# A long convolution inside a gated mixer: one 2048-point plan against two halves of 1024 with three spectrum products

## The chip, the cores and the metric

The kernel runs on one core of one Trainium2 chip. The core has a matrix engine (PE, whose weight loads are shown apart as PEld), a vector engine (DVE), an activation engine (ACT), a general engine (POOL) and an engine that mostly issues transfers (SP). The metric is the time of one execution in microseconds (us), the median of several runs.

## The reference, cut to what matters

A sequence of 2048 rows with 576 channels is normalised. One branch is a long convolution per channel, with a kernel of 2048 taps that is a sum of 128 decaying complex exponentials. The other branch is an MLP with 4608 hidden units. The product of the two is added to the input.

```python
xn = _layernorm(x, axis=-1)
# A: K[d, l] = 2 Re sum_n C[d, n] exp(A[d, n] dt[d] l),  l = 0..2047
Kf = jnp.fft.rfft(K, L2)                  # L2 = 2 * 2048
Uf = jnp.fft.rfft(u_t, L2)                # u_t = xn, transposed to (channel, time)
y = jnp.fft.irfft(Uf * Kf[None], L2)[:, :, :L]
s = y + xn * D_skip
# B: MLP with w1 (576 x 4608), w2 (4608 x 576)
g = _silu(gelu(_layernorm(xn) @ w1 + b1) @ w2 + b2)
return x + s * g
```

## The kernel before, in words

**The MLP** is the larger part of the matrix work. It runs in 48 slots (12 groups of 384 hidden units, two blocks of 512 rows, two halves of the sequence). Each slot has three first-layer units (`layer1`, line 547, 14 matmuls of 512 columns each) and eight second-layer units (`layer2`, line 604, matmuls of 288 columns). Operands are split in a high and a low part, so that three products give nearly full precision. The hidden units pass through ACT (lines 580 and 583) and DVE (line 586, tile `hl`) before the second layer can read them; DVE also adds the second layer's sums into `acc` (line 612) and makes the low parts of the weights (line 524). These matmuls use the PSUM tiles `mxa` and `mxb`, two banks each.

**The convolution** goes over the channels in six chunks of 96. It uses the other four banks, as two tiles named `cv`.

- The kernel's taps come from tables: for 16 channels at a time (36 times), `tables` builds the exponentials on DVE and ACT from packed parameters `par` (lines 822 to 882; the phases are 128 x 1040 elements, from 65 positions and 16 channels), and `kgen` (line 921) multiplies them on PE into `kt`.
- `k1` (line 1022) and `x1` (line 991) are the first transform stage, of the kernel's taps and of the input `xc`. Each runs twice in a chunk, for 48 channels. `k1` is eight matmuls with 32 rows and 128 columns of weights, 384 columns of data, in four row groups, two matmuls after another in each. `x1` is four matmuls of 64 rows by 128 columns, in two row groups, again two in each. Both fill four banks; DVE empties them with four 32 x 32 block transposes (lines 1027 and 1000), 12 channels at a time.
- `s2` (line 1049) is the second stage, four times a chunk, with matrices `f2t` loaded by SP from the scratch tensor `f2q`. It leaves two halves of the spectrum. ACT copies the kernel's spectrum to `kk` (line 1058); `prod` (line 1064) multiplies each half of the input's spectrum with the same half of the kernel's, in two DVE instructions of 384 columns, and `sums` (lines 1070 and 1071) makes complex products of them in two instructions of 192 columns. This happens twice for each `s2`: 48 sets in all.
- `inverse` (line 1093, twice a chunk, matrices `g2t`), `back` (line 1104) and `i1` (line 1119, matrix `g1t`) transform back; ACT copies the result and POOL stores it to `s_s` (line 1128).

An fp32 matmul shows as two instructions in the profile, each with its weight load.

**Preparation.** Before the first chunk, POOL, DVE and ACT turn the constant matrices into the wanted layout: `load_consts`, `load_turns` and `odd_rows` (first-stage matrices), `order_f2`, `load_f2` and `store_f2` (second stage: 16 ACT copies, line 331, between loads and stores through `f2p` and `f2q`; stores at line 336), and `order_mats` (32 small transfers, line 314, for the inverse). The chunk's first step waits for the mark `f2s` 7, the last of these stores, for `odd`, for the packed parameters, and for three tables.

**What sets the order.** `Order` is a planner in the program itself. It keeps a clock for each engine, with a written-down duration for each step, and puts the convolution's steps, tables and loads between those of the MLP. Each MLP step on ACT and DVE has a due time, and another step goes in only if it ends before the next due time. The order so made is then pinned: each engine executes in that order. A PE step of the convolution goes in after an MLP unit, when the planner's clock says that its inputs are there. One `kgen` may ride with another convolution stage (`ride`). Chunk steps are also spaced by `pace`, which aims at an end at 1060 of the planner's clock.

**The end.** `combine` (lines 641 to 653) works off the first half of the rows, channels 0 to 383 after chunk 3, and the rest after chunk 5; `last_x` and `last_s` (line 664) load what `finish` (lines 678 to 696) needs for the last eight row blocks.

Of the kernel before, what the change touches and what calls it, by code (L numbers as in the profile page):

```python
# [9 lines left out]
F32 = mybir.dt.float32  # L10
# [16 lines left out]
NV = 65  # L27
NM = 96
E1, E8, E64, E512 = 2, 10, 18, 26
# [178 lines left out]
def mixer_kernel(ctx, tc, u, log_a_real, a_imag, c_real, c_imag, log_dt, d_skip, w1, b1, w2, b2,  # L208
# [29 lines left out]
    f2p = dr.tile([P, 32 * P], F32, name="f2p")  # L238
    f2q = dr.tile([P, 32, 2, 32], F32, name="f2q")
    g2p = dr.tile([P, 8, 2, 2, 2, 32], F32, name="g2p")  # L240
    turns_s = dr.tile([2, 32], F32, name="turns_s")
# [8 lines left out]
    f1t = sb.tile([P, 2, 2, 64], F32, name="f1t")  # L250
    g1t = sb.tile([P, 32, 2], F32, name="g1t")
# [6 lines left out]
    TMP = {}  # L258

    def load_tv():  # L260
        nc.sync.dma_start(tv[:, :33], dram(tvals, 0, [[0, P], [1, 33]]))
        nc.sync.dma_start(tv[:, 33:], dram(tvals, 0, [[0, P], [1, 32]]))

    def load_consts(g):
        if g == 0:
            m = sb.tile([P, 2, 2, CH], F32, name="kk").rearrange("p a b c -> p (a b c)")
            for k, (n, w) in dict(e=(0, 64), t=(64, 64), s=(128, 32), c=(160, 2), o=(192, 128), m=(320, 32),
                                  g=(352, 32)).items():
                TMP[k] = m[:, n:n + w]
            nc.gpsimd.dma_start(dram(turns_s, 0, [[1, 32], [32, 2]]), dram(f2, 32 * 32 * P, [[P, 32], [64, 2]]))  # L270
        r = slice(32 * g, 32 * g + 32)
        h, ri = divmod(g, 2)
        nc.gpsimd.dma_start(TMP["e"][r].rearrange("p (k m) -> p k m", k=2),
                            f1[r].rearrange("p (k m) -> p k m", k=8)[:, g::4, :])
        for k, t in ((ri, TMP["g"]), (1 - ri, TMP["s"])):
            nc.gpsimd.dma_start(t[r], g1[64 * k + 32 * h:64 * k + 32 * h + 32, 32 * h:32 * h + 32])
        nc.gpsimd.dma_start(dsk[32 * g:32 * g + 1, :].rearrange("p (c m) -> p c m", m=12),
                            dram(d_skip, 12 * g, [[0, 1], [48, D // 48], [1, 12]]))

    def load_turns():  # L280
        nc.gpsimd.dma_start(TMP["t"], dram(turns_s, 0, [[0, P], [1, 64]]))
        for g in range(4):
            nc.gpsimd.dma_start(TMP["c"][32 * g:32 * g + 32], dram(turns_s, 0, [[1, 32], [32, 2]]))

    def odd_rows():

        e, t, sw, c, o, m, ev = (TMP[k] for k in "etscomg")
        V = nc.vector  # L290
        k = lambda x: x.rearrange("p (r k) -> p r k", r=2)
        V.tensor_mul(k(o[:, :64]), k(e), bc(t[:, :32], 1, 2))
        V.tensor_mul(m, e[:, 32:], t[:, 32:])
        V.tensor_sub(o[:, :32], o[:, :32], m)
        V.tensor_mul(m, e[:, :32], t[:, 32:])
        V.tensor_add(o[:, 32:64], o[:, 32:64], m)
        V.tensor_scalar(o[:, 64:], o[:, :64], -1.0, None, op0=OP.mult)
        for g in range(4):
            r = slice(32 * g, 32 * g + 32)
            V.tensor_copy(f1t[r, g % 2], bc(e[r], 1, 2))  # L300
            V.tensor_copy(f1t[r, 1 - g % 2].rearrange("p a b -> p (a b)"), o[r])
        V.tensor_scalar(c[64:], c[64:], -1.0, None, op0=OP.mult)
        for g in (0, 2):
            r = slice(32 * g, 32 * g + 32)
            V.tensor_scalar(c[r, 1:], c[r, 1:], -1.0, None, op0=OP.mult)
        V.tensor_scalar(sw, sw, c[:, 1:], None, op0=OP.mult)
        V.tensor_copy(g1t[:, :, 0], ev)
        V.scalar_tensor_tensor(g1t[:, :, 1], ev, c[:, :1], sw, op0=OP.mult, op1=OP.add)

    def order_mats(j):  # L310
        hi, ri, half = j // 4, j // 2 % 2, j % 2
        for q in (2 * half, 2 * half + 1):
            for part in range(2):
                nc.gpsimd.dma_start(g2p[32 * q:32 * q + 32, :, hi, ri, part], dram(
                    g2, (64 * ri + hi) * 32 * P + q * P + 64 * part, [[2 * 32 * P, 32], [4 * P, 8], [1, 32]]))

    def order_f2(f):
        for ri in range(2):
            nc.gpsimd.dma_start(f2p[64 * f + 32 * ri:64 * f + 32 * ri + 32, :], f2[64 * ri:64 * ri + 32, :])

    F2 = {}

    def load_f2(k):
        x = sb.tile([P, 2, 2, 2, 64], F32, name="g2t", bufs=2).rearrange("p a b c d -> p (a b c d)")
        nc.gpsimd.dma_start(x, f2p[:, 4 * k * P:4 * (k + 1) * P])

        def part(f):
            if f == 0 and k % 2 == 0:
                F2[0] = sb.tile([P, 8, 64], F32, name="f2t").rearrange("p k (r m) -> p k r m", r=2)
            r = slice(64 * f, 64 * f + 64)  # L330
            nc.scalar.activation(F2[0][r, k % 2 * 4:k % 2 * 4 + 4],
                                 x.rearrange("p (k r m f) -> p f k r m", k=4, r=2, f=2)[r, f], AF.Copy)
        return part

    def store_f2(k):
        nc.gpsimd.dma_start(f2q[:, 4 * k:4 * k + 8], F2[0])

# [1230 lines left out]
```

## Time and profile before

| | |
|---|---|
| median of three runs | 1129.78 us (1127.95 to 1130.93) |
| the profiled execution | span 1127.8 us from the first to the last instruction; its own time is not given apart from that |
| PE busy | 1106.5 us |
| PEld busy | 954.9 us |
| DVE busy | 879.0 us |
| ACT busy | 667.8 us |
| POOL busy | 183.7 us |

Busy times are those of the profile: one execution, taken by the hardware profiler. A matmul's duration in it contains a part in which the next one already runs, so that the sum of the durations of a group is far above its busy time where matmuls run side by side in the array.

### The profile page before, as it was taken

Reading aid. Unit: us, or ns where it says so; the run is one execution under the profiler, and the core shown is the slowest. Engines: PE = TensorE matmul, PEld = TensorE weight load, DVE = VectorE, ACT = ScalarE, POOL = GpSimd, SP = SyncE. Lnnn points to the kernel's source line nnn. Section 1 sums busy time; section 2 is a strip of 40 time slices with the busy share of each in tenths; the row PEclk is TensorE's granted clock in tenths of the full one; section 3 lists DMA queues with packets and bytes.
Section 4 is the critical chain, followed back from the end, with each engine's and each line's share of the span. In section 5 each row is a group of like instructions: output and inputs, shape, how many; then the busy total and the mean of one; then the engine's idle time right before and its main releaser. Section 6 shows DMA issues by size and latency. Waiting matters only on the chain.

```text
span 1127.8 us, 26832 instructions
## 1 busy us (share of the span) xinstructions
PE 1106.5 (98%) x11355; PEld 954.9 (85%) x11355; DVE 879.0 (78%) x1477; ACT 667.8 (59%) x1016; POOL 183.7 (16%) x256
## 2 busy tenths in 40 slices
PE   8999999999999999999999999999999999999997
PEld 7888989988888888878888788888887888889896
DVE  7687578799999889889988779998998465544456
ACT  6486589976667566656777736774657133242333
POOL 5447201134102000010110100000001001122300
PEclk9999999999999999999999999999999999999999
DMA  8535635635454233243351421522232335363413
GB/s 247 207 128 146 214 132 182 190 94 124 131 148 142 59 104 71 86 103 104 125 140 42 105 67 57 128 76 62 88 87 80 103 116 147 92 188 109 132 52 85
DMA packets 110809, 132.39 MB, mean 117 GB/s; under 512 B 59669, under 2 KB 77921, under 8 KB 110113
## 3 DMA queue, kind: packets, MB, share of 16 engines
q1 hardware_dynamic: 95728, 79.59, 25.6%
q0 software_dynamic: 14400, 50.20, 14.1%
q8 instruction: 89, 1.46, 0.5%
q10 hardware_dynamic: 560, 0.89, 0.3%
q14 instruction: 32, 0.25, 0.1%
HBM read 101.87 MB, written 36.63 MB: 123 GB/s over the span
## 4 chain that ended last, share of the span: by engine, by line
PE 80%; DVE 10%; DMA 5%; issue 2%; ACT 2%; POOL 0%; SPq 0%; DVEq 0%; ACTq 0%; POOLq 0%
PE mxb L604 18%; PE mxa L604 18%; PE mxa L547 17%; PE mxb L547 16%; PE cv L921 3%; PE cv L1049 3%; PE cv L1093 2%; DMA par<-par_s 2%; PE cv L1022 2%; PE cv L1119 2%; PE cv L991 1%; DVE acc L612 1%; DMA f2p<-in_f_dram 1%; DVE hl L586 1%; DVE w2l L524 1%
## 5 line engine op out<-in xcount | busy, mean ns | idle before, releaser
L586 DVE TENSOR_TENSOR hl<-h,hh 128x512 fp32r<-128x512 f32 x144 | 98.5, 688 | 134.6 <-ACT hh L583 134.2
L604 PE MATMUL mxa<-w2h,hh 128*128 128x288 f32 x573 | 171.4, 299 | 1.7 <-DVE acc L612 1.3
L604 PE MATMUL mxb<-w2h,hh 128*128 128x288 f32 x576 | 171.8, 298 | 0.1
L604 PE MATMUL mxa<-w2h,hl 128*128 128x288 f32 x573 | 169.7, 296 | 2.0 <-DVE hl L586 1.8
L604 PE MATMUL mxb<-w2h,hl 128*128 128x288 f32 x576 | 170.0, 295 | 0.5 <-DVE hl L586 0.4
L604 PE MATMUL mxb<-w2l,hh 128*128 128x288 f32 x576 | 169.6, 294 | 0.0
L604 PE MATMUL mxa<-w2l,hh 128*128 128x288 f32 x573 | 168.7, 294 | 0.0
L580 ACT ACTIVATE h<-mxa,b1t 128x512 f32<-128x512 f32 x73 | 50.1, 688 | 147.0 <-PE mxa L547 143.3
L604 PEld LDWEIGHTS mxa<-w2h,hh 128*128 128x128 f32 x573 | 107.6, 188 | 9.5 <-issue 3.9
L604 PEld LDWEIGHTS mxb<-w2h,hh 128*128 128x128 f32 x576 | 108.1, 188 | 7.8 <-issue 2.7
L604 PEld LDWEIGHTS mxa<-w2h,hl 128*128 128x128 f32 x573 | 107.5, 188 | 3.5 <-DVE hl L586 3.5
L604 PEld LDWEIGHTS mxb<-w2l,hh 128*128 128x128 f32 x576 | 108.2, 188 | 0.7
L604 PEld LDWEIGHTS mxb<-w2h,hl 128*128 128x128 f32 x576 | 108.1, 188 | 0.7 <-DVE hl L586 0.7
L604 PEld LDWEIGHTS mxa<-w2l,hh 128*128 128x128 f32 x573 | 107.6, 188 | 0.6
L822 POOL DMA_DIRECT2D par<-par_s x36 | 27.4, 763 | 429.2 <-DVE mg L865 428.3
L527 ACT ACTIVATE w2h<-raw 128x576 fp32r<-128x576 f32 x72 | 44.9, 676 | 85.9 <-PE mxa L604 85.2
L583 ACT ACTIVATE hh<-h 128x512 fp32r<-128x512 f32 x144 | 90.5, 630 | 3.7
L580 ACT ACTIVATE h<-mxb,b1t 128x512 f32<-128x512 f32 x71 | 48.9, 689 | 69.5 <-PE mxb L547 67.6
L612 DVE TENSOR_TENSOR acc<-mxb,acc 128x576 f32<-128x576 f32 x88 | 66.1, 751 | 24.8 <-PE mxb L604 24.3
L612 DVE TENSOR_TENSOR acc<-mxa,acc 128x576 f32<-128x576 f32 x88 | 65.8, 748 | 24.6 <-PE mxa L604 24.4
L547 PE MATMUL mxa<-XH,w1h 128*128 128x512 f32 x284 | 78.7, 399 | 1.3 <-DVE acc L612 1.3
L547 PE MATMUL mxb<-XH,w1h 128*128 128x512 f32 x280 | 78.6, 402 | 1.2 <-ACT h L580 1.1
(249 smaller groups left out, 2436.6 us busy)
## 6 DMA issues: line engine op xcount, KB each, us to landing
raw<-in_B_w_dram SPq DMA_DIRECT2D x72, 288.0 KB, 3.6
raw<-in_B_w_dram SPq DMA_DIRECT2D x96, 192.0 KB, 3.0
par_s<-A POOLq DMA_DIRECT2D x4, 2160.0 KB, 8.4
par<-par_s POOLq DMA_DIRECT2D x36, 240.0 KB, 4.3
f2t<-f2q SPq DMA_DIRECT2D x24, 256.0 KB, 3.6
g2t<-g2p SPq DMA_DIRECT2D x24, 256.0 KB, 3.8
raw<-in_B_w_dram SPq DMA_DIRECT2D x48, 96.0 KB, 4.2
xc<-xn_s SPq DMA_DIRECT2D x48, 96.0 KB, 3.9
```

The costliest lines, as they stand in the source:

```text
L527: nc.scalar.activation(h, r, AF.Copy)
L547: nc.tensor.matmul(q, a, b, start=j == 0, stop=j == len(ops) - 1)
L580: nc.scalar.activation(t, q, AF.Gelu_apprx_tanh, bias=b1t[:, g * G + i:g * G + i + 1], scale=1.0)
L583: LAST[0] = nc.scalar.activation(hh[:, i], t, AF.Copy)
L586: nc.vector.tensor_sub(hl[:, i], t, hh[:, i].bitcast(F32))
L604: nc.tensor.matmul(q[:, dh, :288], a[:, i, c], b[:, i, d], start=i == 0 and k == 0, stop=i == G - 1 and k == 2)
L612: nc.vector.tensor_add(o, q[:, dh:dh + n, :288], b if g == 0 else o)
L822: nc.gpsimd.dma_start(PAR[b].rearrange("p (g i) k -> p g (i k)", g=4), dram(par_s, (b // 3 * 48 + b % 3 * 4) * NPAR, [[D * NPAR, P], [12 * ...
L921: nc.tensor.matmul(q[32 * g:32 * g + 32, i // 2, i % 2 * 64:i % 2 * 64 + 64], U[:, ri, 4 * g + i, :], v[:, ri, 4 * g + i, :], start=ri == ...
L1022: nc.tensor.matmul(Q[g // 2 * 2][:, g % 2], f1t[r, (e + g) % 2].rearrange("p f k -> p (f k)"), KT[c, i][r, :, 32 * e:32 * e + 32], start=e ...
L1049: nc.tensor.matmul(Q[i][32 * q:32 * q + 32, f, 2 * ri:2 * ri + 2], m[r, 4 * i + q, 32 * ri:32 * ri + 32], A2[r, 4 * p + 2 * i + q // 2, :, ...
L1093: nc.tensor.matmul(QI[q // 2][64 * f:64 * f + 64, q % 2, i], MAT["g2t", p + i // 2][r, i % 2, f, ri], YS[p + i // 2][0][r, i % 2, ri, f], ...
```

## The change

The sequence is split in two halves of 1024, input and kernel alike. Each half is transformed by itself, 32 by 32 points, with all frequencies shifted by a quarter, so that the part of a product that runs over the end of the half comes out as the imaginary part. The first half of the result is the real part of (input half 0 times kernel half 0). The second half is the imaginary part of that product, and the real part of (half 0 times half 1 plus half 1 times half 0). That makes three complex products where there were two.

- `forward` takes the place of the matmuls of `k1` and `x1`. Each stage is now eight matmuls of 32 rows by 64 columns of weights and 384 columns of data: four row groups, two column halves (one for each half of the sequence), one matmul in each of the eight array tiles. Number and shape of the four transposes after it stay.
- `prod` and `sums` are now five DVE instructions: one product of 768 columns (input half 0 with both kernel halves), one of 384 (input half 1 with kernel half 0), a sum of 384 columns in SBUF, and the two of 192 columns.
- `s2`, `inverse` and `i1` issue as many matmuls of the same shapes as before; `g2t` is half as large. `kgen` is unchanged.
- The tables have 64 positions instead of 65, and other positions: 32a + 527.5 and 527.5 - j.
- Preparation: `load_turns`, `load_f2` and `store_f2` go, `odd_rows` is a single instruction, `order_f2` writes `f2q` directly in eight transfers, `load_g2` and `store_g2` reorder the inverse matrices with four ACT copies, 32 loads and four stores. The first chunk now waits for the last of these stores (`mats` 3).
- `xc` is loaded once per chunk, in eight transfers at its start, instead of twice in four transfers, the second set after the first `x1`.
- The planner's durations: X1 1.7 to 1.1, products 0.95 to 1.4, sums 0.63 to 1.1, the waits of `last_x` 9 to 4, those of `last_s` 8 to 7 for the first and 3 for the others.

```diff
-NV = 65
+NV = 64
...
-    f1t = sb.tile([P, 2, 2, 64], F32, name="f1t")
-    g1t = sb.tile([P, 32, 2], F32, name="g1t")
+    f1t = sb.tile([P, 2, 32], F32, name="f1t")
+    g1t = sb.tile([P, 2, 32], F32, name="g1t")
...
+    def order_f2(j):
+        f, ri = divmod(j, 2)
+        for part in range(2):
+            nc.gpsimd.dma_start(f2q[32 * j:32 * j + 32, :, part], dram(
+                f2, 64 * ri * 32 * P + 64 * part, [[2 * 32 * P, 32], [P, 32], [1, 32]]))
...
+    def load_g2(k):
+        x = sb.tile([P, 2, 2, 2, 64], F32, name="f2t")
+        for q in range(4):
+            for ri in range(2):
+                nc.gpsimd.dma_start(x[32 * q:32 * q + 32, :, ri].rearrange("p i s b -> p i (s b)"), dram(
+                    g2, (64 * ri * 32 + 8 * k + q) * P, [[32 * P, 32], [4 * P, 2], [1, P]]))
...
-    X1, S2, INV, I1, KG = 1.7, 1.75, 2.15, 3.05, 1.03
+    X1, S2, INV, I1, KG = 1.1, 1.75, 2.15, 3.05, 1.03
...
+        def load():
+            XC[0] = sb.tile([P, 2, 32, 24], F32, name="xc", bufs=NXC)
+            for g in range(4):
+                for f in range(2):
+                    nc.sync.dma_start(XC[0][32 * g:32 * g + 32, f], dram(
+                        xn_s, HALF * f * D + c * CH + 24 * g, [[32 * D, 32], [D, 32], [1, 24]]))
...
+        def forward(i, x, rhs, order):
+
+            q = [bank2("cv") for _ in range(2)]
+            Q1ST[i, x] = [t[:, :, :384].rearrange("p g (d b) -> p g d b", b=32) for t in q]
+            lead(q[1])
+            for f in range(2):
+                for g in range(4):
+                    r = slice(32 * g, 32 * g + 32)
+                    nc.tensor.matmul(Q1ST[i, x][g // 2][64 * f:64 * f + 64, g % 2].rearrange(order),
+                                     f1t[r].rearrange("p s k -> p (s k)"), rhs(r, f), start=True, stop=True,
+                                     skip_group_check=True)
...
+            add("DVE", 0.2, skip, need=kt + ([("i1", c - 1)] if c else [("pack", D // PK - 1), ("mats", 3), "odd"] if i == 0 else []))
...
-                PR[i] = sb.tile([P, 2, 4 * CH], F32, name="pr").rearrange("p t (a b d) -> p t a b d", a=2, b=2)
-                for t in range(2):
-                    nc.vector.tensor_mul(PR[i][:, t], bc(Q[i][:, t, 0::2], 2, 2), bc(KK[i][:, t], 1, 2))
+                PR[i] = sb.tile([P, 2, 4 * CH], F32, name="pr").rearrange("p a (f d) -> p a f d", f=4)
+                nc.vector.tensor_mul(PR[i], bc(Q[i][:, 0, 0::2], 2, 4),
+                                     bc(KK[i].rearrange("p f b d -> p (f b) d"), 1, 2))
+                nc.vector.tensor_mul(Y[0][:, i], bc(Q[i][:, 1, 0::2], 2, 2), bc(KK[i][:, 0], 1, 2))
...
-                x, y = PR[i], Y[0]
-                nc.vector.tensor_sub(y[:, i, 0], x[:, :, 0, 0], x[:, :, 1, 1])
-                nc.vector.tensor_add(y[:, i, 1], x[:, :, 0, 1], x[:, :, 1, 0])
+                x, y = PR[i].rearrange("p a (f b) d -> p a f b d", f=2), Y[0]
+                nc.vector.tensor_add(PR[i][:, :, 2:], PR[i][:, :, 2:], y[:, i])
+                nc.vector.tensor_sub(y[:, i, 0], x[:, 0, :, 0], x[:, 1, :, 1])
+                nc.vector.tensor_add(y[:, i, 1], x[:, 0, :, 1], x[:, 1, :, 0])
...
-                two.append(step("DVE", 0.95, lambda i=i: prod(i), cv=-1))
-                two.append(step("DVE", 0.63, lambda i=i: sums(i), mark=("sum", c, p) if i else None))
+                two.append(step("DVE", 1.4, lambda i=i: prod(i), cv=-1))
+                two.append(step("DVE", 1.1, lambda i=i: sums(i), mark=("sum", c, p) if i else None))
...
-        tl["steps"].append(step(None, 9.0, lambda k=k: last_x(k), need=[("kg", NB - 1), ("u", NT - 1)], mark=("x8", k)))
+        tl["steps"].append(step(None, 4.0, lambda k=k: last_x(k), need=[("kg", NB - 1), ("u", NT - 1)], mark=("x8", k)))
...
-        c3["steps"].append(step(None, 8.0, lambda k=k: last_s(k), need=[("st", NCH - 1), ("x8", k)], mark=("s8", k)))
+        c3["steps"].append(step(None, 7.0 if k == 0 else 3.0, lambda k=k: last_s(k), need=[("st", NCH - 1), ("x8", k)], mark=("s8", k)))
```

215 lines of the change are left out of this document (66 added, 149 removed).

## The prediction

> **What bounds the kernel now.** First the page: its head, the busy times, the slices and the chain that ended last.
>
> ```profile
> span 1127.8 us, 26832 instructions
> ...
> PE 1106.5 (98%) x11355; PEld 954.9 (85%) x11355; DVE 879.0 (78%) x1477; ACT 667.8 (59%) x1016; POOL 183.7 (16%) x256
> ...
> PE   8999999999999999999999999999999999999997
> ...
> DVE  7687578799999889889988779998998465544456
> ...
> POOL 5447201134102000010110100000001001122300
> ...
> PE 80%; DVE 10%; DMA 5%; issue 2%; ACT 2%; POOL 0%; SPq 0%; DVEq 0%; ACTq 0%; POOLq 0%
> ```
>
> PE is busy in every slice, and most of the chain is PE. So a microsecond of PE work that goes is a microsecond of time, as long as nothing else comes to keep PE waiting. DVE is the engine to watch: 78% over the whole, but 9 tenths in many slices from the 10th to the 31st. The next view is PE's waits; these are the ones inside the run, without the start's.
>
> ```profile
> PE cv L1093 <- issue: 2.1, 2, 1.3
> PE mxa L604 <- DVE hl L586: 1.8, 4, 0.6
> ...
> PE mxa L547 <- DVE acc L612: 1.3, 1, 1.3
> PE mxa L604 <- DVE acc L612: 1.3, 1, 1.3
> PE mxb L547 <- ACT h L580: 1.1, 2, 0.7
> PE mxb L604 <- DVE hl L586: 0.4, 1, 0.4
> ```
>
> DVE and ACT together cost PE 1.8 + 1.3 + 1.3 + 1.1 + 0.4 = 5.9 us. No row has a convolution stage (tile `cv`) that waits for DVE or for a load: the planner puts a stage in only when its inputs are there. So there is little idle time to win. The gain must come out of PE's own work.
>
> **The first transform stage.** The groups by line give PE's convolution work, and the view of one line the median durations.
>
> ```profile
> L1049 PE MATMUL cv<-A,f2t 64*32 64x192 f32 x1536 | 38.5, 332 | 0.0
> ...
> L1093 PE MATMUL cv<-ys,g2t 32*64 32x96 f32 x1536 | 22.8, 253 | 2.2 <-issue 2.1
> L1022 PE MATMUL cv<-kt,f1t 32*128 32x384 f32 x192 | 18.9, 507 | 0.0
> L991 PE MATMUL cv<-xc,f1t 64*128 64x384 f32 x96 | 18.7, 508 | 0.0
> ```
> ```profile
> L1022 PE MATMUL cv<-kt,f1t x192: 481/481/586, 249.1 to 894.2; 32*128 32x384 f32 x192
> ```
> ```profile
> L1093 PE MATMUL cv<-ys,g2t x1536: 238/241/293, 306.2 to 981.0; 32*64 32x96 f32 x192
> ```
>
> The rows L1022 and L991 are 12 stages each (six chunks, two calls): 18.9 / 12 = 1.57 us and 18.7 / 12 = 1.56 us. From 96 columns to 384 the median grows from 241 to 481 ns, which is 0.833 ns a column; 384 columns stream for 320 ns, and some 161 ns of each duration are a fixed part in which the next matmul already runs. In both stages each array tile now works off two matmuls of two instructions, 4 x 320 ns = 1.28 us, and 0.28 to 0.29 us are filling and draining. After the change there are eight array tiles with one matmul each: 2 x 320 = 0.64 us, and with the same 0.29 us the stage is 0.93 us.
>
> Do eight tiles run side by side, the two column halves of one row group with different data? L1093 does just that: 32 x 64 tiles, 1536 x 80 ns of streaming = 123 us in 22.8 us of busy time, at least 5.4 at once; L1049 has 1536 x 160 ns = 246 us in 38.5 us, 6.4 at once. Both figures count filling and draining. So I take 0.64 us saved per stage; the ends are 0 (the halves come one after the other) and 0.76 us (nothing of the filling left but the fixed 161 ns, so 0.80 us a stage). That this is time on PE's path is seen around one stage, in order of time:
>
> ```profile
> 248.80 0.39 PE L547 MATMUL mxb<-XR,w1s 128*128 128x512 f32 x1
> 249.12 1.57 PE L1022 MATMUL cv<-kt,f1t 32*128 32x384 f32 x16
> 250.62 1.20 PE L547 MATMUL mxa<-XH,w1h 128*128 128x512 f32 x4
> ```
> ```profile
> 1101.50 3.19 PE mxa L547 x14
> ```
>
> From the MLP's last matmul before it to the first after it are 1.82 us. Without the stage these two start about 0.23 us apart (14 of them take 3.19 us in the chain, the last row), so the stage costs 1.59 us, 0.31 us of which is not streaming. That part is for entering and leaving, and the change leaves the number of entries as it is. **The term is 24 x 0.64 = 15.4 us.**
>
> The Trainium skill, page "TensorEngine Tiling (Array Packing)", section "Tiling Modes", says that changing the tiling mode drains the engine. The trace agrees with the 0.31 us above, which speak against halving a stage whole: halving all of its 1.59 us would give 24 x 0.80 = 19 us.
>
> `s2`, `inverse`, `i1` and `kgen` keep their matmuls: 0.
>
> **The products on DVE.** Before: two of 384 columns, two of 192. After: 768, 384, 384 in SBUF, 192, 192.
>
> ```profile
> L1064 DVE TENSOR_TENSOR pr<-cv,kk 128x384 f32<-128x384 f32 x96 | 48.6, 547 | 2.1 <-ACT kk L1058 2.0
> ...
> L865 DVE TENSOR_TENSOR mg<-par 128x1024 f32<-128x1024 f32 x36 | 43.9, 1221 | 0.6
> ...
> L865 DVE TENSOR_TENSOR mg<-par 128x512 f32<-128x512 f32 x36 | 24.6, 682 | 0.0
> ...
> L1070 DVE TENSOR_TENSOR ys<-pr 128x192 f32<-128x192 f32 x48 | 17.0, 355 | 1.1
> ```
>
> No row has 768 columns; between 512 (682 ns) and 1024 (1221 ns) lie 1.05 ns a column, so 952 ns. A set goes from 2 x 547 + 2 x 355 = 1804 ns to 952 + 2 x 547 + 2 x 355 = 2756 ns. In the order of time a set takes less, since the next instruction starts before the last has ended:
>
> ```profile
> 290.37 1.01 DVE L1064 TENSOR_TENSOR pr<-cv,kk 128x384 f32<-128x384 f32 x2
> 291.42 0.36 DVE L1070 TENSOR_TENSOR ys<-pr 128x192 f32<-128x192 f32 x1
> ...
> 291.69 0.35 DVE L1071 TENSOR_TENSOR ys<-pr 128x192 f32<-128x192 f32 x1
> ...
> 291.96 0.75 DVE L612 TENSOR_TENSOR acc<-mxb,acc 128x576 f32<-128x576 f32 x1
> ```
>
> That is 1.59 us, 0.05 us less for each of four instructions. With the same for five, a set grows by 0.90 us, and 48 sets by 43 us, to about 922 us of DVE in a shorter run, 83%. What hides it is DVE's idle time:
>
> ```profile
> 250.00:870.00 620.00, 614.24 (x7662) 520.48 (x7655) 553.25 (x911) 398.92 (x550) 56.19 (x85) 1.00 0.35 96
> 870.00:995.00 125.00, 124.90 (x1244) 105.08 (x1243) 67.08 (x123) 41.34 (x68) 16.75 (x29) 1.00 0.39 113
> ```
>
> (Columns: stretch, length, then busy PE, PEld, DVE, ACT, POOL, granted clock, share and rate of the transfers.) In the stretch with tables and chunks DVE is busy 553 of 620 us. 80 of the 96 products of L1064 start in it, so 40 sets and 36 us more against 67 us of idle time. It fits only as an average: behind each product on DVE stand the hidden layer's low part (L586) and the sums that free `mxa` and `mxb` (L612), and PE waits for both. The planner's durations for the two steps (1.4 and 1.1 us) are about what I find (2.5 us), so it sees the load and moves chunks later rather than delay the MLP. The present waits of 5.9 us may stay (0) or double (5.9 us); I take **1.6 us more**, nearer to the waits that DVE causes today at 89%, since the stretch can lengthen. If that cover were gone, all 43 us would land on PE.
>
> **Moved work, at nothing.** The chunks may end later: 36 us of DVE at 89% is up to 40 us. Two places absorb it.
>
> ```profile
> 221.62 0.36 ACT L926 ACTIVATE kt<-cv 128x256 f32<-128x256 f32 x1
> ```
> ```profile
> 243.79 0.56 POOL L336 DMA_DIRECT2D f2q<-f2t x1 [8.84 <-ACT f2t L331]
> ```
>
> The third table of chunk 0 is there at 222, but the first stage starts at 249.12, after the last `f2q` store at 243.79: the reordering, which waits for ACT's 16 copies, holds it for 27 us. The new preparation has four copies in place of 16; its eight `f2q` transfers, 36 of POOL's for the inverse and the wait for `mats` 3 come in their place, and POOL, idle through most of slices 5 to 9 (113 to 254 us), has room for them. If it is done by 222, chunk 0 starts up to 27 us earlier; if not, nothing is lost before the next place, the end:
>
> ```profile
> 994.46 0.90 POOL L1128 DMA_DIRECT2D s_s<-ys x1 [0.42 <-ACT ys L1127]
> ```
> ```profile
> 1049.67 0.58 SPq L664 DMA_DIRECT2D A<-s_s x1
> ```
> ```profile
> 1097.45 0.75 DVE L685 TENSOR_TENSOR A<-A,acc 128x576 f32<-128x576 f32 x1
> ```
>
> The last result of the convolution is stored at 995, the last of its loads is issued at 1050, and the first use of such a load is at 1097: 47 us of slack, 15 less after the change, plus what the shorter waits of `last_s` give (64 us of planned waits become 28). A delay of up to 40 us is covered; beyond some 60 us each microsecond would count.
>
> ```profile
> SPq L966 <- PE cv L991: 71.7, 6, 27.9
> ```
>
> SP's waits show what the loads of `xc` do now: the second set stands in the queue until `x1` has read the first, with weight loads behind it. With one load for a chunk this goes, and PE, which waits for no weight load now, gains nothing. The smaller tables and matrices cost nothing.
>
> **The sum.** 1127.8 - 15.4 + 1.6 = 1114.0 us for the span. The median is 2.0 us above the profiled span, so 1116.0 us.
>
> **The rivals.** Measurement can tell about 0.3%, 3.4 us, from no change.
>
> *The shorter stage brings nothing.* Either the column halves run one after the other (1.57 us a stage as now), or emptying `cv` sets the pace: four transposes follow each stage.
>
> ```profile
> L1027 DVE STREAM_TRANSPOSE A<-cv 128x384 f32<-128x384 f32 x48 | 24.3, 553 | 2.2 <-PE cv L1022 2.2
> ```
>
> They take 4 x 553 = 2.2 us, more than either 0.93 or 1.57. Against it: L1093 shows the halves side by side, and PE works for the MLP in other banks while `cv` is emptied. It gives 1129.8 + 1.6 = 1131.4 us. The Trainium skill, the same page, section "PSUM Bottleneck", says that tiling speeds up the matmuls but not the emptying of PSUM; the trace has the transposes slower than the stage already, and no wait of PE for them.
>
> *DVE's order gives much of it back.* Where 6 to 12 of the 48 sets delay an MLP step by their 0.90 us, 5.4 to 10.8 us return: 1119.8 to 1125.2 us, taken at 1122.
>
> *Slower: DVE becomes what PE waits for.* The place is the stretch from 250 to 870, where the product stands in front of L586 or L612. The price is 0.90 us a set; it decides from 15.4 / 0.90 = 17 sets of 48 on. At 28 sets, 25.2 us return, and the time is 1129.8 - 15.4 + 25.2 = 1139.6 us; at all 48, 1157.6 us. For it speaks 89% DVE; against it, that only 5.9 us of waits are there at that load, and that the planner knows the new durations.
>
> **Chances.** The forecast, 1112 to 1119.8 us: 0.72. Much given back: 0.13. Nothing from the stage: 0.06. Slower: 0.09. So faster by over 0.3% 0.85, within 0.3% 0.06, slower 0.09. The range of 8 in 10 takes the forecast and most of the second case, and below the forecast the lower end of a stage (24 x 0.76 = 18.2 us and no new wait: 1111.6 us): 1111 to 1124 us.
>
> **What would show it.** The new stage's groups at 0.93 us each, 22 us together instead of 37.6; PE's busy time near 1091 us; DVE near 920 us, with products of 0.95 and 0.55 us; rows of PE's waits for `hl`, `acc` and `h` together under 8 us; the first stage before 249, the last store of `s_s` by 1035. Stages at 1.5 us, or waits for L586 and L612 of 15 us and more, would make the prediction wrong.

## The result, and the profile after

The changed kernel takes 1109.91 us, the median of four runs (1109.69 to 1111.96), against 1130.36 us for the kernel before, measured beside it (1127.95 to 1131.19): a ratio of 0.983, with an interval of 0.9816 to 0.9844. It is 20.4 us faster. The profiled span went from 1127.8 to 1107.5 us, 20.3 us less. The forecast was 1116.0 us in a range of 1111 to 1124, so the direction is right and the median lies 1.1 us below the range.

From the page of the changed kernel, the head, the busy times, the slices of PE and DVE, and the shares of the chain that ended last:

```profile
span 1107.5 us, 27061 instructions
...
PE 1087.3 (98%) x11451; PEld 944.0 (85%) x11451; DVE 917.3 (83%) x1508; ACT 670.0 (60%) x1012; POOL 178.3 (16%) x244
...
PE   8999999999999999999999999999999999999997
...
DVE  7787566787799999998999988899899998676457
...
PE 86%; DVE 6%; ACT 4%; DMA 2%; issue 1%; SPq 0%; DVEq 0%; ACTq 0%
```

PE lost 19.2 us of busy time and DVE gained 38.3 us, and PE's share of the chain rose from 80 to 86%. DVE's nines now reach to the 33rd slice, where before they ended at the 30th: the convolution ends later.

PE's groups for the convolution, by line (busy time, mean ns of one, then idle time before them):

```profile
L996 PE MATMUL cv<-A,f2t 64*32 64x192 f32 x1536 | 38.5, 332 | 0.0
L1042 PE MATMUL cv<-ys,g2t 32*64 32x96 f32 x1536 | 22.2, 253 | 2.2 <-issue 2.2
L958 PE MATMUL cv<-kt,f1t 32*64 32x384 f32 x192 | 10.9, 506 | 1.7 <-DVE kt L970 1.7
L958 PE MATMUL cv<-xc,f1t 32*64 32x384 f32 x192 | 10.8, 507 | 0.0
```

The two rows of L958 are the new first stage: 21.7 us where the two stages took 37.6, so 0.90 us each instead of 1.57. The other stages have not moved. PE's waits inside the run:

```profile
PE cv L1042 <- issue: 2.2, 1, 2.2
PE mxb L511 <- ACT h L544: 1.9, 2, 1.5
PE cv L958 <- DVE kt L970: 1.7, 1, 1.7
PE mxb L568 <- DVE hl L550: 1.6, 1, 1.6
PE mxa L568 <- DVE acc L576: 0.9, 2, 0.6
PE mxa L568 <- DVE hl L550: 0.8, 2, 0.6
```

The waits for `hl`, `acc` and `h` are 1.9 + 1.6 + 0.9 + 0.8 = 5.2 us; before they were 5.9. The products on DVE:

```profile
L1012 DVE TENSOR_TENSOR pr<-cv,kk 128x768 f32<-128x768 f32 x48 | 45.6, 950 | 0.5 <-ACT kk L1005 0.5
L1018 DVE TENSOR_TENSOR pr<-pr,ys 128x384 f32<-128x384 f32 x48 | 26.5, 553 | 0.6
L1014 DVE TENSOR_TENSOR ys<-cv,kk 128x384 f32<-128x384 f32 x48 | 26.3, 547 | 0.0
```

Each set has the five durations that were expected. Where they went is seen in the same two stretches as before (length, then busy PE, PEld, DVE, ACT, POOL, granted clock, share and rate of the transfers):

```profile
250.00:870.00 620.00, 615.35 (x7420) 529.58 (x7419) 565.01 (x908) 397.49 (x552) 35.59 (x49) 1.00 0.30 84
870.00:995.00 125.00, 124.70 (x1469) 107.16 (x1468) 101.34 (x174) 56.39 (x84) 23.04 (x41) 1.00 0.51 141
```

In the long stretch DVE rose only from 553 to 565 us, 91%. In the next one it rose from 67 to 101 us. The row of L1012 for the long stretch alone counts 36 sets, where it was 40 with the kernel before, although the first stage now starts earlier:

```profile
L1012 DVE TENSOR_TENSOR pr<-cv,kk 128x768 f32<-128x768 f32 x36 | 34.2, 950 | 0.5 <-ACT kk L1005 0.5
```
```profile
226.51 1.00 PE L958 MATMUL cv<-kt,f1t 32*64 32x384 f32 x16 [1.68 <-DVE kt L970]
```

The second fence is the first stage of chunk 0 in the order of time, at 226.5 us (249.1 before). The end of the convolution, by the rows of tile `s_s` (durations, then first and last start):

```profile
L628 SPq DMA_DIRECT2D A<-s_s x8: 320/427/1214, 1054.1 to 1062.2; - x8
...
L1077 POOL DMA_DIRECT2D s_s<-ys x6: 890/894/902, 409.6 to 1050.4; - x6
```

The last result is stored at 1050.4 us, 56 us later than before, in a program that is 20 us shorter.

**The account of PE.** The starts of all PE matmuls, in order, add up to the span. Between two MLP matmuls that follow each other directly the usual pitch is 0.2265 us (512 columns) or 0.1322 us (288 columns); these pitches make 913.4 us in every kernel here. "Visits" is the time from an MLP matmul to the next one with convolution or preparation stages between them, less that pitch. "Gaps" is what two neighbouring MLP matmuls take beyond it. "Start" is everything ahead of the first MLP matmul, "tail" all that follows the last matmul's start.

| kernel | span | visits | gaps | start | tail |
|---|---|---|---|---|---|
| before | 1127.8 | 167.6 | 26.3 | 13.0 | 7.6 |
| after | 1107.5 | 152.3 | 20.8 | 13.5 | 7.6 |

So of the 20.3 us, 15.3 come from the visits, 5.5 from the gaps, and the start gives back 0.5. Of the 5.5 us, 1.9 lie in the first 45 us. The gaps hold the named waits, many short delays, and in some runs matmuls at a lower granted clock. The visits hold waits too: in the changed kernel the 1.7 us for `kt` in front of the first stage of chunk 0.

### The profile page after: what moved, and what is told of

It is laid out like the page before. It is cut to its first block, busy times and chain, and to the rows that moved or that the text cites. A ratio compares the mean times of both kernels' runs of the same rounds, so it can differ in the third digit from the quotient of the medians.

```text
span 1107.5 us, 27061 instructions
## 1 busy us (share of the span) xinstructions
PE 1087.3 (98%) x11451; PEld 944.0 (85%) x11451; DVE 917.3 (83%) x1508; ACT 670.0 (60%) x1012; POOL 178.3 (16%) x244
## 4 chain that ended last, share of the span: by engine, by line
PE 86%; DVE 6%; ACT 4%; DMA 2%; issue 1%; SPq 0%; DVEq 0%; ACTq 0%
PE mxb L568 19%; PE mxa L568 19%; PE mxa L511 18%; PE mxb L511 18%; PE cv L885 3%; PE cv L996 3%; PE cv L958 2%; PE cv L1068 2%; PE cv L1042 1%; DMA raw<-in_B_w_dram 1%; DMA xc<-xn_s 1%; PE cv L416 1%; DVE acc L576 1%; ACT h L544 1%; DVE hl L550 0%
```

## The experiments

The theory: the shorter first stage is time on PE's path one for one, and it is the gain that the change itself makes; DVE's third product costs nothing because the planner moves convolution steps later, into room at the end. The rivals: the gain comes from the order that the planner happened to make; the third product has a price that something else repaid; the earlier start of chunk 0 is what made room. Every ratio stands against the kernel before, measured beside the run.

| run | median | ratio to before (interval) |
|---|---|---|
| `e1_half_stage` | 1114.72 | 0.986 (0.9842 to 0.9877) |
| `e2_half_stage_told` | 1116.57 | 0.9883 (0.9868 to 0.9899) |
| `e3_stage_twice` | 1128.17 | 0.9993 (0.998 to 1.0005) |
| `e4_longer_products` | 1126.48 | 0.997 (0.9951 to 0.9989) |
| `e5_planner_not_told` | 1142.99 | 1.0124 (1.0101 to 1.0146) |
| `e6_late_start` | 1119.75 | 0.9911 (0.9892 to 0.9931) |
| `e7_more_dve` | 1168.42 | 1.0345 (1.0329 to 1.0361) |
| `e8_two_products` | 1113.02 | 0.9852 (0.9832 to 0.9871) |
| `e9_unchanged` | 1106.93 | 0.9819 (0.9801 to 0.9838) |
| `e10_told_1_0` | 1109.06 | 0.9829 (0.9814 to 0.9843) |
| `e11_told_1_2` | 1114.10 | 0.9877 (0.9862 to 0.9891) |
| `e12_told_products` | 1119.86 | 0.9925 (0.991 to 0.9939) |

**The stage alone: `e1_half_stage` and `e2_half_stage_told`.** Both are the kernel before with half of the first stage's matmuls; in the second the planner knows of it as well (last part of the diff).

```diff
-                for e in range(2):
-                    for g in range(4):
-                        r = slice(32 * g, 32 * g + 32)
-                        nc.tensor.matmul(Q[g // 2 * 2][:, g % 2], f1t[r, (e + g) % 2].rearrange("p f k -> p (f k)"),
-                                         KT[c, i][r, :, 32 * e:32 * e + 32], start=e == 0, stop=e == 1,
-                                         skip_group_check=True)
+                for g in range(4):
+                    r = slice(32 * g, 32 * g + 32)
+                    nc.tensor.matmul(Q[g // 2 * 2][:, g % 2], f1t[r, g % 2].rearrange("p f k -> p (f k)"),
+                                     KT[c, i][r, :, :32], start=True, stop=True, skip_group_check=True)
...
-                        r = slice(64 * v, 64 * v + 64)
+                        r = slice(64 * v + 32 * e, 64 * v + 32 * e + 32)
...
-    X1, S2, INV, I1, KG = 1.7, 1.75, 2.15, 3.05, 1.03
+    X1, S2, INV, I1, KG = 1.1, 1.75, 2.15, 3.05, 1.03
```

> The kernel before, with half of the first transform stage left out: one matmul in each of the four row groups in place of two (for the input only 32 of the 64 rows that belong to each output, for the taps only one of the two summands). The planner's durations are untouched, so the order of every engine is that of before. Theory (the gain is streaming time that goes from PE's path): two instructions of 320 ns less in each array tile, 24 stages, 15.4 to 16 us less, near 1114.5 us, and the two groups fall from 37.6 to about 22 us. Rival (some 4 us of the 20 us come with the shorter stage itself, in entering and leaving it): 19 to 21 us less, near 1110 us. Rival (the gain comes from the other order): under 5 us.

> As e1_half_stage, half of the first stage left out, and the planner is told 1.1 us for the stage in place of 1.7, so that it orders anew. Theory: the order adds little, 0 to 2 us less than e1_half_stage, near 1113 us. Rival (the 4 us beyond the stage come from the new order: other neighbours, other waits): near 1110 us, 4 us less than e1_half_stage.

The groups of `e1_half_stage`:

```profile
L1021 PE MATMUL cv<-kt,f1t 32*128 32x384 f32 x96 | 11.1, 533 | 0.0
L991 PE MATMUL cv<-xc,f1t 32*128 32x384 f32 x96 | 11.1, 533 | 0.0
```

The two stages take 22.2 us, 15.4 less than before, and the time falls by 14.7 us, with the order of all instructions as it was. In the account the visits go from 167.6 to 152.2 us, just as in the changed kernel (152.3), while the gaps stay near before's (27.6). So the first stage is worth its own length, and it explains the visits' 15.3 us but not the 5.5 us of the gaps. With the planner told, the same work in another order is 1.9 us slower than `e1_half_stage`, at the edge of the two intervals, and the waits have grown:

```profile
PE mxa L604 <- DVE hl L586: 6.1, 7, 2.0
```

That row was 1.8 us in the kernel before: a better figure for the planner did not make a better order.

**The stage lengthened again: `e3_stage_twice`.** The changed kernel, each first-stage matmul issued twice, the planner told.

```diff
-            for f in range(2):
+            for f in (0, 1, 0, 1):
...
-    X1, S2, INV, I1, KG = 1.1,
+    X1, S2, INV, I1, KG = 1.75,
```

> The changed kernel, with all eight matmuls of each first stage issued twice (the second time over the same result), and the planner told 1.75 us. Theory: streaming time is on PE's path one to one, 24 x 0.64 = 15.4 us more than the changed kernel, near 1125 us. Rival (the gain came from the order, the preparation or the start, not from the stage): under 5 us more.

The groups show the second round:

```profile
L958 PE MATMUL cv<-xc,f1t 32*64 32x384 f32 x384 | 19.4, 494 | 0.1
L958 PE MATMUL cv<-kt,f1t 32*64 32x384 f32 x384 | 18.7, 494 | 0.0
```

These are 38.1 us, 16.4 more than in the changed kernel; the visits are 168.1 us, 15.8 more, and the time is back at that of the kernel before. The median is 18.3 us above that of the changed kernel, 3 more than the stage term, which was expected. All that else changed, the three products, the new preparation and the single load of `xc`, gives no gain here that can be told from nothing, as far as one order of the work can show it.

**The products alone: `e4_longer_products`.** The kernel before, with two DVE instructions of 384 columns more in each set, and the changed kernel's two durations for products and sums in the planner.

```diff
                     nc.vector.tensor_mul(PR[i][:, t], bc(Q[i][:, t, 0::2], 2, 2), bc(KK[i][:, t], 1, 2))
+                nc.vector.tensor_max(PR[i][:, 0], PR[i][:, 0], PR[i][:, 0])
...
                 x, y = PR[i], Y[0]
+                nc.vector.tensor_max(x[:, 1], x[:, 1], x[:, 1])
...
-                two.append(step("DVE", 0.95, lambda i=i: prod(i), cv=-1))
-                two.append(step("DVE", 0.63, lambda i=i: sums(i), mark=("sum", c, p) if i else None))
+                two.append(step("DVE", 1.4, lambda i=i: prod(i), cv=-1))
+                two.append(step("DVE", 1.1, lambda i=i: sums(i), mark=("sum", c, p) if i else None))
```

> The kernel before, with the change's DVE load alone: two more DVE instructions of 384 columns in each of the 48 product sets (a maximum of a tile with itself), about 0.95 us a set, and the planner told the change's durations, 1.4 and 1.1 us. Theory (DVE's idle time covers it, the chunks end later): 0 to 2 us more than before, near 1131 us, waits of PE for hl, acc and h together under 8 us, the last store of s_s near 1050 instead of 994. Rival (the products delay the MLP's steps): 10 to 45 us more, in PE's waits for hl and acc.

The busy times and the last stores:

```profile
PE 1105.8 (98%) x11355; PEld 954.5 (85%) x11355; DVE 923.0 (82%) x1573; ACT 673.8 (60%) x1020; POOL 184.0 (16%) x256
```
```profile
L1130 POOL DMA_DIRECT2D s_s<-ys x6: 892/894/927, 368.1 to 1059.1; - x6
```

DVE has 44 us more to do (923.0 against 879.0), the convolution ends 65 us later (1059.1 against 994.5), and the time doesn't rise: the ratio is 0.997, its interval just below 1. The load is paid at the end of the convolution, where there is room.

**The planner not told: `e5_planner_not_told`.** The changed kernel with the planner's durations of the kernel before; the three figures were put back together and not told apart.

```diff
-    X1, S2, INV, I1, KG = 1.1,
+    X1, S2, INV, I1, KG = 1.7,
...
-                two.append(step("DVE", 1.4, lambda i=i: prod(i), cv=-1))
-                two.append(step("DVE", 1.1, lambda i=i: sums(i), mark=("sum", c, p) if i else None))
+                two.append(step("DVE", 0.95, lambda i=i: prod(i), cv=-1))
+                two.append(step("DVE", 0.63, lambda i=i: sums(i), mark=("sum", c, p) if i else None))
```

> The changed kernel, with the planner still counting the durations of before (1.7 us for the first stage, 0.95 and 0.63 us for products and sums). The work is the same, only the order differs. Theory (the planner's knowledge is what keeps 43 us of DVE work out of the MLP's way): waits of PE for hl, acc and h grow from 5.2 us to 10 us and more, 4 to 15 us more than the changed kernel, 1114 to 1125 us. Rival (DVE has room anyway): within 2 us of the changed kernel, near 1110 us.

The same instructions take 1142.99 us, 33 more than the changed kernel (4 to 15 were expected) and 1.2% more than the kernel before. The chain and PE's waits, then one of them in DVE's order of time, and PE's first matmul after it:

```profile
PE 62%; DVE 26%; ACT 5%; issue 4%; DMA 3%; SPq 0%; DVEq 0%; ACTq 0%; POOLq 0%
```
```profile
PE mxa L568 <- DVE acc L576: 10.5, 8, 3.1
PE mxb L568 <- DVE hl L550: 5.0, 4, 1.7
PE mxb L568 <- DVE acc L576: 3.8, 6, 1.6
```
```profile
887.13 0.95 DVE L1012 TENSOR_TENSOR pr<-cv,kk 128x768 f32<-128x768 f32 x1
888.00 0.55 DVE L1014 TENSOR_TENSOR ys<-cv,kk 128x384 f32<-128x384 f32 x1
888.58 0.56 DVE L1018 TENSOR_TENSOR pr<-pr,ys 128x384 f32<-128x384 f32 x1
...
889.72 1.22 DVE L813 TENSOR_TENSOR w<-w 128x1024 f32<-128x1024 f32 x1
890.85 0.75 DVE L576 TENSOR_TENSOR acc<-mxa,acc 128x576 f32<-128x576 f32 x1
```
```profile
891.66 0.40 PE L568 MATMUL mxa<-w2h,hh 128*128 128x288 f32 x1 [3.07 <-DVE acc L576]
```

A set of 2.6 us and a table's step of 1.2 us stand in front of the sum that frees `mxa`, and PE waits 3.07 us. In the account the gaps are 50.7 us, 29.9 more than in the changed kernel, and the visits 3.2 more. Some 5 us of this are not waits: three stretches (375 to 380, 745 to 750 and 890 to 895 us), behind waits of 3.0, 1.6 and 3.1 us, have a granted clock of 0.66 to 0.70, which costs about 1.7 us each, as the last section shows. This is the rival on the slower side, in the place and by the mechanism that the prediction named. What keeps it out of the changed kernel is the planner's knowledge of the new durations; that it is the products' durations alone, and not also that of the first stage, this run doesn't show.

**The start of chunk 0: `e6_late_start`.** The changed kernel, with chunk 0 held back to about where it began before.

```diff
             add("DVE", 0.2, skip, need=kt + (... [("pack", D // PK - 1), ("mats", 3), "odd"] if i == 0 else []),
+                at=0.0 if c or i else 246.0)
```

> The changed kernel, with the first chunk held back until about the time at which it starts before the change (near 249 us instead of 226). Theory (DVE's load sets the pace of the tables, so the early start is worth nothing): the last store of s_s stays between 1040 and 1060, the time within 2 us of the changed kernel. Rival A (each us of the start counts at the end): the store comes near 1073, its loads after their first use, 5 to 10 us more. Rival B (the early start with few tables is itself what makes the first chunk long and the end late): the store comes before 1025.

It takes 9.8 us more than the changed kernel (12.3 us in the profiled execution), but not at the end. The last store is only 8.5 us later (1058.9) and the tail only 0.6 us longer. The rest is in the account's visits (156.7, 4.4 more), its gaps (26.5, 5.7 more) and its start (15.0, 1.5 more); some 3.4 us of it are two stretches of lower clock. The first result is even stored earlier than in the changed kernel, at 379.1 against 409.6 us. None of the three outcomes that were written down came. So an early start of chunk 0 doesn't fix the end of the convolution, and this run can't say what the start is worth: it shows only one more order.

**More and less on DVE: `e7_more_dve` and `e8_two_products`.** The changed kernel with one more DVE instruction of 768 columns in each set, and with two products in place of three; the planner told in both.

```diff
                 x, y = PR[i].rearrange("p a (f b) d -> p a f b d", f=2), Y[0]
+                nc.vector.tensor_max(PR[i], PR[i], PR[i])
...
-                two.append(step("DVE", 1.1, lambda i=i: sums(i), mark=("sum", c, p) if i else None))
+                two.append(step("DVE", 1.97, lambda i=i: sums(i), mark=("sum", c, p) if i else None))
```
```diff
-                nc.vector.tensor_mul(PR[i], bc(Q[i][:, 0, 0::2], 2, 4),
-                                     bc(KK[i].rearrange("p f b d -> p (f b) d"), 1, 2))
-                nc.vector.tensor_mul(Y[0][:, i], bc(Q[i][:, 1, 0::2], 2, 2), bc(KK[i][:, 0], 1, 2))
+                for f in range(2):
+                    nc.vector.tensor_mul(PR[i][:, :, 2 * f:2 * f + 2], bc(Q[i][:, f, 0::2], 2, 2), bc(KK[i][:, f], 1, 2))
...
-                nc.vector.tensor_add(PR[i][:, :, 2:], PR[i][:, :, 2:], y[:, i])
...
-                two.append(step("DVE", 1.4, lambda i=i: prod(i), cv=-1))
-                two.append(step("DVE", 1.1, lambda i=i: sums(i), mark=("sum", c, p) if i else None))
+                two.append(step("DVE", 0.95, lambda i=i: prod(i), cv=-1))
+                two.append(step("DVE", 0.63, lambda i=i: sums(i), mark=("sum", c, p) if i else None))
```

> The changed kernel, with one more DVE instruction of 768 columns in each of the 48 product sets (a maximum of a tile with itself, 0.95 us), and the planner told of it. Theory (DVE's load is paid at the end, once the slack behind the last store of s_s is used up, which is 15 us now): the last store goes from 1050 to 1090 or later, 20 to 50 us more than the changed kernel, while PE's waits for hl, acc and h inside the run stay under 10 us. Rival (it is still covered): under 3 us more. Rival (it is paid inside the run): PE's waits for hl, acc and h grow by 15 us and more.

> The changed kernel with two of the three spectrum products (the cross products of the second half are left out, half 1 times half 1 takes their place), so with DVE's product instructions as they were before, and the planner told 0.95 and 0.63 us. Theory (the third product costs nothing because it is covered): 0 to 2 us less than the changed kernel, near 1109 us, the last store of s_s 30 us or more earlier. Rival (the third product costs PE something): 4 us and more less.

`e8_two_products` has 42 us less on DVE (874.9) and isn't faster: 1113.02 us, its interval overlapping that of the changed kernel. Its last store comes at 1029.8 us, 20.6 earlier and not the 30 that were expected. With `e4_longer_products`, the third product is free to within what one order differs from another. One more instruction of 0.95 us is not: 58.5 us more, above the 20 to 50 that were expected and above the 43 us by which DVE's busy time grew (960.3). The last store and a late step of DVE in `e7_more_dve`:

```profile
L1078 POOL DMA_DIRECT2D s_s<-ys x6: 887/892/900, 423.3 to 1115.8; - x6
```
```profile
1124.30 0.76 DVE L649 TENSOR_TENSOR A<-A,acc 128x576 f32<-128x576 f32 x1 [15.23 <-DMA A<-s_s]
```

PE's waits for `hl`, `acc` and `h` ahead of MLP matmuls are still only 5.5 us inside the run. The convolution ends at 1116, after the MLP, and `finish` then waits for its loads. So with the planner told, too much DVE work is not paid as waits of the MLP but all at once, at the end.

**How much lies in the order: `e9_unchanged` to `e12_told_products`.** The changed kernel again; the same with X1 at 1.0 and at 1.2 instead of 1.1; and with the products' steps at 1.5 and 1.2 instead of 1.4 and 1.1. The work is the same in all four. The first diff is that of `e10_told_1_0` (1.2 in its place in `e11_told_1_2`), the second that of `e12_told_products`.

```diff
-    X1, S2, INV, I1, KG = 1.1,
+    X1, S2, INV, I1, KG = 1.0,
```
```diff
-                two.append(step("DVE", 1.4, lambda i=i: prod(i), cv=-1))
-                two.append(step("DVE", 1.1, lambda i=i: sums(i), mark=("sum", c, p) if i else None))
+                two.append(step("DVE", 1.5, lambda i=i: prod(i), cv=-1))
+                two.append(step("DVE", 1.2, lambda i=i: sums(i), mark=("sum", c, p) if i else None))
```

> The changed kernel itself once more, beside the next three. Theory (the profile's gain is 15.3 us of convolution stages and 5.5 us of fewer waits and slow matmuls between the MLP's own, which belong to the order and so come again): 1108.5 to 1111.5 us, and the time between the MLP's matmuls beyond their pitch again near 20.8 us. Rival (the 5.5 us are chance of one execution): that time between 23 and 27 us in this profile, and a median of 1112 us or more.

> The changed kernel, the planner told 1.0 us for the first stage in place of 1.1. Same work, another order. Theory (what a planned order costs in waits scatters by several us from one order to the next): 1107 to 1120 us, the first stage's two groups again 21.7 us, the rest in waits. Rival (the waits follow DVE's load, which is the same): within 1.5 us of e9_unchanged.

> The changed kernel, the planner told 1.2 us for the first stage in place of 1.1. Same work, another order. Theory (scatter of the order): 1107 to 1120 us, not the same as e10_told_1_0 by more than 2 us. Rival (the waits follow DVE's load): within 1.5 us of e9_unchanged.

> The changed kernel, the planner told 1.5 and 1.2 us for products and sums, which is what the profile shows (0.95 + 0.55 and 0.55 + 2 x 0.355 us), in place of 1.4 and 1.1. Same work. Theory (scatter of the order, and a little less waiting since the durations are truer): 1106 to 1118 us. Rival (truer durations take out the remaining waits for hl and acc, 3.3 us): 1105 to 1107 us, faster than the changed kernel.

| run | span | visits | gaps | start | tail | last store of `s_s` | last `combine` on DVE |
|---|---|---|---|---|---|---|---|
| `e9_unchanged` | 1104.4 | 150.0 | 20.5 | 12.9 | 7.6 | 1047.3 | 1091.5 |
| `e11_told_1_2` | 1112.1 | 152.4 | 24.7 | 12.9 | 8.7 | 1058.7 | 1102.0 |
| `e12_told_products` | 1117.6 | 151.1 | 21.9 | 13.0 | 18.2 | 1065.7 | 1107.2 |

The same program as the changed kernel came out 3.0 us lower in `e9_unchanged` (1.2 us by the ratios), below what was expected. Its gaps came again; its visits are 2.3 us less, and there PE doesn't wait for `kt` in front of the first stage. So the visits fell by 15.3 us in one execution and by 17.6 in the other, and the account is good to some 2 us. The chosen figures gave the best of the four orders. `e10_told_1_0` can't be told from `e9_unchanged`; `e11_told_1_2` is 7.2 us slower, 4.2 of them in the gaps and 1.1 in the tail; `e12_told_products`, whose durations are truer, is 12.9 us slower, at 1119.86 us where at most 1118 was expected; 10.6 us of it are in the tail. DVE's last `combine` in `e12_told_products`, in the order of time, and then the rows of tile `row` for the changed kernel and for the kernel before (first and last start):

```profile
1107.24 0.56 DVE L613 TENSOR_TENSOR row<-row 128x384 f32<-128x384 f32 x1 [3.50 <-DMA row<-g_s]
```
```profile
L613 DVE TENSOR_TENSOR row<-row x11: 526/551/748, 893.1 to 1094.6; 128x384 f32<-128x384 f32 x9, 128x576 f32<-128x576 f32 x2
```
```profile
L649 DVE TENSOR_TENSOR row<-row x11: 547/551/750, 929.0 to 1080.8; 128x384 f32<-128x384 f32 x9, 128x576 f32<-128x576 f32 x2
```

In `e12_told_products` this `combine` is the last work on DVE, and 10.4 us lie between its start and the end of the span. In `e11_told_1_2` it is 10.1 us, and the chain that ended last runs through it on DVE, ahead of the last steps of `finish`. In the changed kernel 1107.5 - 1094.6 = 12.9 us, and its chain has no `combine` at the end: by estimate about 2.5 us of room are left. None of these versions is faster than the changed kernel.

## The prediction, step by step

**What bounds the kernel: right.** PE bounds it, and a microsecond of PE's work that went was a microsecond of time (`e1_half_stage`, `e3_stage_twice`). The slices in which DVE shows 9 tenths run from the 9th to the 30th, not from the 10th to the 31st; nothing rests on that.

**The first stage, 24 x 0.64 = 15.4 us: right.** The groups fell by 15.9 us, 0.66 a stage, to the forecast 22 us together, and the visits by 15.3. The column halves do run side by side with different data, and nearly all of the 0.31 us for entering and leaving stayed: a stage that stands alone between MLP matmuls costs 0.92 us of path in `e9_unchanged`, on the mean of 14, where it was 1.59 on the mean of 17; 0.92 - 0.64 leaves 0.28. At 0.67 us a stage the term was 16.1 us; the visits fell by 15.3 with the new wait of 1.7 us for `kt` in them, and by 17.6 in `e9_unchanged` without it. So the rival that the shorter stage brings nothing is out, in both of its forms.

**The products, 43 us of DVE covered: right in size, and the reason holds, but not by the room that was named.** DVE grew by 38 us in all, to 917 in place of 922, and by 44 for the like load in `e4_longer_products`, and the time didn't feel it. The prediction let 36 us more go into the 67 idle microseconds of the stretch from 250 to 870. Only 12 went in. The planner held DVE at 91% there and put four sets and later tables behind it. That it sees the load and moves chunks rather than delay the MLP was the sentence that decided: `e5_planner_not_told` shows the slower rival, at 33 us, which is 33 / 0.90 = 37 sets' worth, above the break-even of 17.

**The waits, 1.6 us more: the step that failed.** The prediction took the waits to follow DVE's load. The gaps went down by 5.5 us instead of up by 1.6. That difference of 7.1 us is the whole miss: the visits fell by 0.1 us less than the stage term, the start gave back 0.5, and the median lies 2.4 us above the profiled span instead of 2.0, so that -7.1 + 0.1 + 0.5 + 0.4 = -6.1 us. DVE's load is not what sets this term. In the same work under neighbouring orders the gaps lie between 20.5 and 24.7 us, in `e8_two_products`, with less load, at 23.0, and in `e4_longer_products`, with more, at 23.9. Of the 5.5 us, 1.9 are ahead of 45 us; a wait of PE for the load of `w` at the start, 1.6 us, is gone. The other 3.6 us are within what orders differ by, so a forecast of this term to 2 us was not to be had from DVE's load, and that the total came out on the good side of the forecast is luck of the order. The time of the rival in which DVE's order gives much back is near that of `e12_told_products`, 1119.86, but there it is lost at the end and not in waits of the MLP. What in an order makes for few gaps stays open.

**Moved work, at nothing: right in its sum, wrong in its limits.** The first stage started before 249, as said. The last store came at 1050, not by 1035: 44 us of DVE moved the end by 65 us in `e4_longer_products`. The load didn't raise DVE's share in the long stretch there (549 us in place of 553), which fits the planner's rule that other steps go in only where the MLP's due times let them. And the limit at the end was not the first use of the loads of `A`, which is set by the MLP's own last sums: `e4_longer_products` issues them up to 1115 us and its tail is 8.7 us, 1.1 more. The limit is the last `combine` (in `e7_more_dve`, far past the room, the chain runs through these loads and the `combine`). In the kernel before it started at 1080.8, 47 us ahead of the end, of which 10.4 are needed, so 36.6 us were free; 2.5 of them are left. That is the room of the `combine` where it stood; the store had more. From the last store to this `combine` are 86.3 us in the kernel before, 44.2 in the changed kernel, 41.5 in `e12_told_products` and 40.5 in `e7_more_dve`, so about 45 us were free there too. By this estimate the store had some 80 us of room in all, not 60, and the changed kernel uses 76 of them: its store comes 56 us later in a span 20 us shorter. The rest fits `e12_told_products`, whose store is 15.3 us later and whose tail is 10.6 us longer. The shorter waits of `last_s` did what was said (from the last store to the last load it is now 12 us, before it was 55), but the kernel with the old waits was not tried. One such step more on DVE, or a planner that is a little more careful, and the end is late.

## What to carry to other kernels

Where an engine bounds the whole run, measure a shorter stage by its own groups and believe it one for one, but price the added work on the other engines by where the schedule will push it: look for the last thing that depends on it and count the room there, through every step to the end. A planner's written durations are part of the change; with the old ones this gain is a loss of 1.2%. And run the same work under a few neighbouring orders before reading anything into the last half per cent: here they spread over 13 us.

## What the runs showed of the hardware

Short idle gaps of PE can cost more than their length. In `e6_late_start` PE waits 2.02 us for `h`, and the windows around it (length, busy PE, granted clock, share and rate of the transfers) show a lower clock behind it:

```profile
754.92 0.40 PE L568 MATMUL mxb<-w2h,hh 128*128 128x288 f32 x1 [2.02 <-ACT h L544]
```
```profile
750.00:755.00 5.00, 2.98 (x19) 1.00 0.00 0
755.00:760.00 5.00, 5.00 (x134) 0.66 0.18 52
```

A mean of 0.66 over 5 us leaves out 1.7 us of full clock, beside the wait's own two. With PE idle for long, in `e7_more_dve` from 1120 to 1165 us, the granted clock is 0.50; at that clock 1.7 us lost are a stretch of 3.4 us. `e8_two_products` has the same behind a wait of 2.08 us (0.79 and 0.87 in two neighbouring windows). It doesn't come behind every such wait. In the same run, `e6_late_start`, an equal one keeps 1.00:

```profile
467.17 0.41 PE L568 MATMUL mxb<-w2h,hh 128*128 128x288 f32 x1 [2.02 <-ACT h L544]
```
```profile
470.00:475.00 5.00, 5.00 (x72) 1.00 0.54 101
```

The changed kernel's longest wait, 2.2 us, keeps 1.00 too, and so does one of 1.98 us in `e2_half_stage_told`. On the other side, the 745 us stretch of `e5_planner_not_told` follows a wait of only 1.63 us. The length of one wait doesn't decide it in these runs; what does stays open. The Trainium skill, page "TensorE: Matmul & The Clock Gate", section "What's actually happening", says that the half clock comes after an idle window of about 3.4 us; these runs show it after gaps of 1.6 to 3.1 us, and not after every one, and the measurement decides. The kernel before and the changed kernel have no such stretch before their last matmuls; that is one more way in which an order with few long waits is worth more than their sum.
